# Chunk squares in wider products, router loads, block 0's norms and two Q Grams moved, in a delta-rule attention with top-1 experts

## The chip, the cores and the metric

The kernel runs on one core of one Trainium2 chip. The metric is device time in microseconds, the median of several executions. TensorE does matrix products, VectorE and ScalarE elementwise work and copies out of PSUM, GpSimd (POOL in the profile) masks, copies inside SBUF and indirect DMAs, and SyncE (SP) issues the plain DMAs from one queue, in order.

## The reference, cut to what matters

```
# attention: B, H, S, D = 4, 8, 768, 48
k_n = k / (norm(k) + 1e-06)
state = 0                                   # per (b, h): D x D
for t in range(S):
    y[:, :, t] = q_t @ state                # einsum 'bhd,bhde->bhe'
    v_old = state^T k_t                     # einsum 'bhde,bhd->bhe'
    state += beta_t * outer(k_t, v_t - v_old)
# mixture of experts on x = y as (3072 tokens, 384 features); E = 8 experts, F = 1024
logits = x @ w_gate;  e = argmax(logits);  gate = softmax(logits)[e]
out = gate * (relu(x @ w1[e]) @ w2[e])
```

## The kernel before, in words

The sequence is cut into six blocks of 128 positions; a block of one batch entry is a chunk, numbered n = 4 * block + batch, 24 in all, each with eight heads. `kt_t[n]` holds the keys of a chunk by feature, two heads above each other (rows 0 and 64), and `qt_t[n]` the queries.

For each chunk, `kpart(n)` (L229) forms the Gram of keys (`halves`, L265: eight products with 64 rows and 128 columns, one per head, into two PSUM tiles of the ring "g", which has three buffers) and ScalarE copies both to `gg` (L253). `qpart(n)` (L275) does the same with keys and queries, and GpSimd then masks the result `pm` (L282). Inside a chunk the delta rule is solved in four sub-blocks of 32 positions, for which the 32x32 diagonal blocks of the Gram of all 32 batch-head pairs are inverted at once on VectorE: `prepare(tb)` (L301) takes the squared norms (`squares`), the root on ScalarE (`root`, L298) and the scaling, and `lanes(tb)` (L357) runs the columns of the inverse, then products and reductions (L393, L399), and a last transpose to `wt`. Blocks 1 to 5 get their diagonals by way of DRAM (`gd`, `lg`), from the Grams. Block 0 can't wait for that: the first step of `kpart` for chunks 0 to 3 computes its diagonal blocks alone, the squares, with 32 products of 32 columns for each chunk (L246), which VectorE and ScalarE copy to `dg` (L248, L249), each taking the heads of one half.

Then come 27 ticks. In tick t, `residual(t)` subtracts from the scaled values `v_all` what the states and the earlier sub-blocks give (L434, L446 on TensorE, L453 on VectorE), `apply(t)` multiplies with `wt` (L461), ScalarE copies the result to `u` (L465), and `finish(t - 3)` updates the state and emits the output of a finished chunk, whose tokens go through the router's columns of `esel` (L528). Between these, `beside(t, i)` puts a measured portion of the later blocks' inverses on VectorE; one more K Gram (chunk t + 12) and one Q Gram are formed in each tick. `norms(tb)` (L338) brings the norms into `nt_all`, one column for each head, and `scale_v(t)` (L409) scales a tick's values with them. The experts' products follow behind the ticks and fill the rest of the time.

The order on each engine is that of the program text: the schedule is written by hand. Ahead of the ticks (L869 and after) it is: loads of chunks 0 to 3, dummy products, the steps in `INIT` (first steps of chunks 0 to 3, one step of block 0's `prepare`, the Gram of chunk 0), `constants()` on GpSimd, which ends with the four loads of the router's weights into `esel` (L103), then the loads of chunks 4 to 10 and of values on the same queue, the rest of `prepare(0)`, and the Grams in the order of `FILL`, between which stand the columns of block 0's inverse, `norms(0)` and `scale_v(0)`.

Of the kernel before, what the change touches and what calls it, by code (L numbers as in the profile page):

```python
# [8 lines left out]
F32 = mybir.dt.float32  # L9
# [9 lines left out]
B, H, S, D = 4, 8, 768, 48  # L19
C = 128  # L20
NT = S // C
NB = C // 32
BH = B * H
NP = H // 2
# [17 lines left out]
def deltanet_moe(ctx, tc, kt_d, qt_d, kn_d, v_d, beta_d, w_gate, w1, w2, out):  # L42
    nc = tc.nc
# [27 lines left out]
    def iota(t, pattern, start, step=0):  # L71
        nc.gpsimd.iota(t, pattern=pattern, base=start, channel_multiplier=step, allow_small_or_imprecise_dtypes=True)

    def constants():
        nc.gpsimd.memset(esel, 0.0)
        for p in range(NP):
            for a in range(2):

                r = slice(64 * a, 64 * a + D)
                nc.gpsimd.tensor_copy(esel[r, p, (p + a) % 2 * D:((p + a) % 2 + 1) * D], ident[r, r])  # L80
        cmask = lp.tile([128, 128], F32, name="cmask", tag="u", bufs=UB)
        nc.gpsimd.memset(cmask, 1.0)
        nc.gpsimd.affine_select(out=cmask, in_=cmask, compare_op=ALU.is_gt, fill=0.0, base=0,
                                pattern=[[1, 128]], channel_multiplier=-1)
        nc.gpsimd.tensor_copy(ltri, cmask)
        nc.gpsimd.memset(ones, 1.0)
        iota(last_i, [[1, CAP - 128 * NG]], 128 * NG)
        iota(rev_e, [[-1, E]], E)
        for e in range(E):
            nc.gpsimd.memset(pow_e[:, e:e + 1], float(2 << (E - 1 - e)))  # L90
        iota(base, [[CAP, E]], 0)
        iota(lim, [[CAP, E]], CAP)
        iota(beyond, [[N - CAP, E]], OFF)
        nc.gpsimd.memset(jump, 0.0)
        for i, g in enumerate((G0, NG)):
            nc.gpsimd.memset(jump[:, i, 0:1], float(128 * g))
        iota(ids, [[-C, B * NT]], int(TOPID), -1)
        nc.gpsimd.memset(ids2, 0.0)
        nc.gpsimd.tensor_copy(ids2[:, :, 0], ids)
        wv = w_gate.rearrange("(p a r) e -> a r p e", p=NP, a=2)  # L100
        for a in range(2):
            for o in range(2):
                nc.sync.dma_start(out=esel[64 * a:64 * a + D, o::2, 2 * D:], in_=wv[(a + o) % 2, :, o::2])  # L103

    YB = 2
    KSB = 1
    VA = NT * B - B
    GB = 3
# [7 lines left out]
    NB_ = 2  # L116
    LIVE = 7
    LAG = NB - 1
    FILL = 'k4 k5 k6 k7', 'k1 q0 k2 k3', 'k8 k9', 'k10 k11 q1'

    ROOT = {1: (-1, -1, -1), 2: (17, 20, 22), 3: (38, 41, 43), 4: (66, 69, 71), 5: (94, 97, 99)}
    INIT = (0, 1, 2, 3, 'l', 0)

    STEPS = (3, 3, 3, 2, 2, 2, 2)

# [29 lines left out]
    pss = lp_.enter_context(tc.tile_pool(name="pss", bufs=1, space=PSUM))  # L155
    pg_ = lp_.enter_context(ExitStack())
    psg_ = [pg_.enter_context(tc.tile_pool(name="psg", bufs=GB, space=PSUM))]
# [13 lines left out]
    nt_t = lp.tile([128, (NT * B + LAG) * H], F32, name="nt_all")  # L171
# [16 lines left out]
    def load_rows(t, src, whole):  # L188

        for r in (slice(0, 128),) if whole else (slice(0, D), slice(64, 64 + D)):  # L190
            nc.sync.dma_start(out=t[r], in_=src[r])

    def load_k(n):
        if n < NT * B:
            load_rows(kt_t[n % KTL], kt_d[n], n < KTL)
# [10 lines left out]
    def stage(t):  # L206

        return [(q, t - q) for q in range(NB) if 0 <= t - q < NT * B]
# [20 lines left out]
    def kpart(n):  # L229

        tb, b = n // B, n % B
        kt, gg = kt_t[n % KTL], gg_t[n % KSL]
        V, A = nc.vector.tensor_copy, nc.scalar.copy
        if tb == 0:
            if n == 0:
                tiles["dg"] = fp.tile([128, BH, 32], F32, name="dg", tag="lg", bufs=3)
            dg = tiles["dg"]
            db = [psg_[-1].tile([128, NP, 32], F32, name=f"db{b}_0", tag="g"),
                  pss.tile([128, NP, 32], F32, name=f"db{b}_1", tag="y", bufs=YB) if b < 2 else
                  pss.tile([128, NP, 32], F32, name=f"db{b}_1", tag=f"sum{b - 2}")]  # L240
            for h in range(H):
                p, a = h // 2, h % 2
                r = slice(64 * a, 64 * a + 64)
                for i in range(NB):
                    t = slice(32 * i, 32 * i + 32)
                    nc.tensor.matmul(db[a][t, p, :], lhsT=kt[r, p, t], rhs=kt[r, p, t], start=True, stop=True,  # L246
                                     tile_position=(64 * a, 32 * i), skip_group_check=True)
            V(out=dg[:, b * H:(b + 1) * H:2], in_=db[0])  # L248
            A(out=dg[:, b * H + 1:(b + 1) * H:2], in_=db[1])  # L249
            yield  # L250
        pg = halves(f"pg{tb}_{b}", kt, kt)
        for a in range(2):
            A(out=gg[:, a:H:2], in_=pg[a])  # L253
        if tb > 0 and b == B - 1:
            early_ = CL[tb] if tb < len(CL) else (0, 0)
            clear_slots(early_[0])
            for i in range(NB):
                r = slice(32 * i, 32 * i + 32)
                nc.sync.dma_start(out=gd[tb].rearrange("(i n) (r c) -> i r n c", i=NB, r=32)[i],
                                  in_=gg_g[tb % (KSL // B)].rearrange("p b h c -> p (b h) c")[r, :, r])  # L260
            tiles[tb]["lg"] = fp.tile([128, 32, 32], F32, name=f"lg{tb}", tag="lg", bufs=3)
            clear_slots(early_[1])
            nc.sync.dma_start(out=tiles[tb]["lg"].rearrange("p r c -> p (r c)"), in_=gd[tb])
# [73 lines left out]

    def norms(tb):  # L338
        s0, s1 = tiles[tb]["s0"], tiles[tb]["r0"]
        if tb > 0:  # L340
            nc.vector.transpose(out=s1, in_=s0)
        for q in range(NB):
            p = slice(32 * q, 32 * q + 32)
            c = slice((B * tb + q) * H, (B * tb + q) * H + 32)
            if tb > 0:
                nc.gpsimd.tensor_copy(nt_t[p, c], s1[p])
            else:
                nc.vector.transpose(out=nt_t[p, c], in_=s0[p])
        yield

    def both_halves(t):
# [57 lines left out]
    def scale_v(t, act=False):  # L409

        vn = vt[t]
        for r in rows(t):
            for h in range(H if act else 0):
                nc.scalar.activation(out=vn[r, h], in_=vn[r, h], func=AF.Copy, scale=nt_t[r, t * H + h:t * H + h + 1])
            if act:
                continue
            nc.vector.tensor_tensor(out=vn[r], in0=vn[r], in1=nt_t[r, t * H:(t + 1) * H].unsqueeze(2)
                                    .broadcast_to([r.stop - r.start, H, D]), op=ALU.mult)
# [9 lines left out]
    def residual(t):  # L428

        ks = tiles["ks", t] = pss.tile([128, H, D], F32, name=f"ks{t}", tag="ks", bufs=KSB)  # L430
        st = stage(t)
# [37 lines left out]
    def finish(n):  # L469
# [4 lines left out]
        qt, pm = qt_t[n % QTL], pm_t[n % QSL]  # L474
        yp = [pss.tile([128, NP // 2, C], F32, name=f"yp{tb}_{b}_0", tag="y", bufs=YB),
              psg_[-1].tile([128, NP // 2, C], F32, name=f"yp{tb}_{b}_1", tag="g")]
# [47 lines left out]
    def emit_x(n, yt, row, rl):  # L524

        xp = pss.tile([128, NP, 2 * D + E], F32, name=f"xp{n // B}_{n % B}", tag="y", bufs=YB)
        for p in range(NP):
# [20 lines left out]
    def emit_slots(tb, b, w, row, rl):  # L548
# [28 lines left out]
        for _ in range(FP if w > 1 else 3):  # L577
            yield
        pp = pss.tile([128, w + 1, E], F32, name=f"pp{tb}_{b}", tag="y", bufs=YB)
        nc.tensor.matmul(pp[:, 0:w, :], lhsT=ltri, rhs=ohb, start=True, stop=False, skip_group_check=True)  # L580
# [42 lines left out]
    def pool_slots(tb, b, w, row, rl):  # L623
# [39 lines left out]
        for _ in range(FP):  # L663
            yield
        pp = pss.tile([128, w + 1, E], F32, name=f"pp{tb}_{b}", tag="y", bufs=YB)
        nc.tensor.matmul(pp[:, 0:w, :], lhsT=ltri, rhs=ohb, start=True, stop=False, skip_group_check=True)
# [42 lines left out]
    def dummy(k):  # L709

        if k:
            wm = pss.tile([128, 512], F32, name=f"wm{next(cnt)}", tag="y", bufs=YB)
        for _ in range(k):
# [171 lines left out]
    lane = prepare(0)  # L885
    for i in INIT:
        if i == "l":
# [21 lines left out]
    def fill(xs):  # L909
        for x in xs.split():  # L910
            n, part = int(x[1:]), (ks0 if x[0] == "k" else qs0)
            if part[n] and not run(part[n]):
                done.add(x)

    fill(FILL[0])
    load_k(3 * B - 1)
# [3 lines left out]
        load_ku(n)  # L920
    for n in range(LEAD, LEAD + 2):
        load_k(n)
    fill(FILL[1])
    lane = lanes(0)
    run(lane, 12)
    for _ in norms(0):
        pass
    scale_v(0)
    run(lane, 24)
    fill(FILL[2])  # L930
    fill(FILL[3])
    ks_ = [x for i, x in enumerate(ks_) if f"k{i}" not in done]
# [128 lines left out]
    i = 0  # L1061
# [87 lines left out]
    V = nc.vector  # L1149
# [93 lines left out]
    if True:  # L1243
# [3 lines left out]
        V = nc.vector  # L1247
# [61 lines left out]
        for f in range(KF):  # L1309
# [4 lines left out]
                                     in_=yo, in_offset=None, bounds_check=N - 1, oob_is_err=False)  # L1314
# [40 lines left out]
```

## Time and profile before

| | |
|---|---|
| median of 3 runs | 496.92 us (496.26 to 499.41) |
| the profiled execution | 496.72 us, span 495.0 us |
| TensorE, products | 453.5 us busy (92%), 7212 |
| TensorE, weight loads | 417.3 us busy (84%), 7212 |
| VectorE | 323.8 us busy (65%), 726 |
| ScalarE | 262.1 us busy (53%), 566 |
| GpSimd | 166.1 us busy (34%), 338 |
| mean granted clock of TensorE | 0.982 |
| DMA | 73.33 MB, mean 148 GB/s |

The span is what the profiler saw of the program from its first to its last instruction; the execution's own time is 1.72 us longer. Busy time is a share of the whole span and hides that the stages have different limits. In rows of a timeline the first number is the start in microseconds from the start of the span, the second the time that the row covers, xN the number of instructions that it merges, and the bracket the idle time of the engine ahead of it with what ended it. A single-precision product appears as two instructions, so the 128 squares of four chunks make 256.

### The profile page before, as it was taken

What the parts mean: (1) busy time and instruction counts of PE and PEld (TensorE: products, weight loads), DVE (VectorE), ACT (ScalarE), POOL (GpSimd) and SP (SyncE); (2) the same over time, 40 slices, a digit from 0 to 9 for tenths busy, and PEclk for the clock granted to TensorE, in tenths of its full rate; (3) what the DMA queues carried; (4) which work ended last, traced back from release to release, by engine and by line L of the source; (5) the groups of instructions that cost most, each with busy time, mean ns of one, the idle gap of its engine ahead of it and who ended that gap; (6) DMA issues with size and microseconds to landing.
All of it is one profiled execution on the core that took longest, in us unless ns stands there. A gap on an engine that the chain in (4) does not pass through costs nothing. (4 is left out here: it accounts for less than half of the span.)

```text
span 495.0 us, 17216 instructions
## 1 busy us (share of the span) xinstructions
PE 453.5 (92%) x7212; PEld 417.3 (84%) x7212; DVE 323.8 (65%) x726; ACT 262.1 (53%) x566; POOL 166.1 (34%) x338
## 2 busy tenths in 40 slices
PE   6866799999999899978899999999999999999995
PEld 4755678887888687866798999999999999999995
DVE  3899998899889989446544767373463647255330
ACT  3464767675756466766433455463553545364230
POOL 7013123768888878730311210201102020201111
PEclk9998889999999999999999899999999999999999
DMA  5999478575384243734302548474545547353101
GB/s 164 246 291 252 126 156 254 169 162 168 88 206 106 86 131 89 234 121 128 101 35 66 168 139 248 140 223 132 177 124 171 175 150 199 138 170 106 36 3 46
DMA packets 57147, 73.33 MB, mean 148 GB/s; under 512 B 25929, under 2 KB 44831, under 8 KB 57056
## 3 DMA queue, kind: packets, MB, share of 16 engines
q1 hardware_dynamic: 53600, 62.44, 44.4%
q0 software_dynamic: 3456, 9.57, 5.3%
q8 instruction: 71, 1.16, 1.0%
q14 instruction: 20, 0.16, 0.1%
HBM read 54.15 MB, written 18.62 MB: 147 GB/s over the span
## 5 line engine op out<-in xcount | busy, mean ns | idle before, releaser
L801 POOL DMA_INDIRECT out_dram<-yo,idx x32 | 30.7, 959 | 198.7 <-ACT yo L1134 100.8
L798 PE MATMUL y<-w2h,hx 128*128 128x384 f32 x352 | 93.5, 340 | 0.1
L721 DVE TENSOR_TENSOR w2l<-w2r,w2h 128x768 fp32r<-128x768 f32 x32 | 31.2, 979 | 73.3 <-ACT w2h L720 73.2
L798 PEld LDWEIGHTS y<-w2h,hx 128*128 128x128 f32 x352 | 64.1, 188 | 0.4 <-issue 0.4
L798 PE MATMUL y<-w2l,hx 128*128 128x384 f32 x176 | 59.3, 337 | 0.0
L787 PE MATMUL h<-xl,w1h 128*128 128x416 f32 (+2 forms) x168 | 57.2, 341 | 0.2 <-DVE xl L721 0.2
L787 PE MATMUL h<-xh,w1h 128*128 128x416 f32 (+2 forms) x168 | 57.3, 341 | 0.0
L787 PE MATMUL h<-xh,w1l 128*128 128x416 f32 (+2 forms) x168 | 57.2, 340 | 0.0
L465 ACT COPY u<-ks 32x384 f32<-32x384 f32 x96 | 45.1, 469 | 21.0 <-PE ks L461 18.4
L282 POOL TENSOR_SCALAR_AFFINE_SELECT pm<-pm 128x1024 f32<-128x1024 f32 x24 | 27.1, 1130 | 75.9 <-ACT pm L281 75.5
L790 ACT ACTIVATE hx<-h 128x448 fp32r<-128x448 f32 (+1 forms) x64 | 32.9, 517 | 32.8 <-PE h L787 32.0
L1134 ACT ACTIVATE yo<-y,gt 128x384 f32<-128x384 f32 x22 | 12.8, 581 | 69.1 <-PE y L798 57.9
L434 PE MATMUL ks<-st,kt 128*32 128x96 f32 x768 | 45.1, 253 | 2.5 <-ACT u L465 2.1
L791 DVE SCALAR_TENSOR_TENSOR hx<-h,hx 128x448 fp32r<-128x448 f32 (+1 forms) x64 | 36.8, 587 | 14.5 <-ACT hx L790 14.4
L271 PE MATMUL pg<-kt 64*128 64x128 f32 x384 | 34.0, 319 | 8.0 <-DMA kt<-in_kt_dram 4.3
L271 PEld LDWEIGHTS pg<-kt 64*128 64x128 f32 x384 | 28.8, 219 | 12.4 <-ACT gg L253 6.4
L434 PEld LDWEIGHTS ks<-st,kt 128*32 128x32 f32 x768 | 33.2, 111 | 6.1 <-ACT u L465 2.6
L253 ACT COPY gg<-pg 128x512 f32<-128x512 f32 x48 | 25.8, 589 | 23.8 <-PE pg L271 23.8
L536 POOL DMA_INDIRECT xg<-row,sli x24 | 29.2, 1216 | 25.7 <-ACT yt L508 8.0
L461 PE MATMUL ks<-v_all,wt 32*32 32x48 f32 x1536 | 25.9, 203 | 12.9 <-DVE v_all L453 10.7
L461 PEld LDWEIGHTS ks<-v_all,wt 32*32 32x32 f32 x1536 | 21.3, 105 | 17.8 <-DVE v_all L453 12.6
L721 DVE TENSOR_TENSOR w1l<-w1r,w1h 128x1024 fp32r<-128x1024 f32 x24 | 29.4, 1224 | 9.8 <-ACT w1h L720 6.6
(197 smaller groups left out, 1040.5 us busy)
## 6 DMA issues: line engine op xcount, KB each, us to landing
w1r<-in_w_dram SPq DMA_DIRECT2D x24, 512.0 KB
w2r<-in_w_dram SPq DMA_DIRECT2D x32, 384.0 KB
xg<-zrow SPq DMA_DIRECT2D x7, 788.0 KB
kt<-in_kt_dram SPq DMA_DIRECT2D x17, 256.0 KB
xr<-xg SPq DMA_DIRECT2D x7, 591.0 KB
ku<-in_kn_dram SPq DMA_DIRECT2D x20, 192.0 KB
qt<-in_qt_dram SPq DMA_DIRECT2D x36, 96.0 KB
v_all<-in_v_dram SPq DMA_DIRECT2D x15, 192.0 KB
```

The source lines that it names most:

```text
L271: nc.tensor.matmul(pg[a][:, p], lhsT=kt[r, p], rhs=xt[r, p], start=True, stop=True, tile_position=(64 * a, 0), skip_group_check=True)
L282: nc.gpsimd.affine_select(out=pm, in_=pm, compare_op=ALU.is_gt, fill=0.0, base=0, pattern=[[0, H], [1, C]], channel_multiplier=-1)
L434: nc.tensor.matmul(ks[32 * q:32 * q + 32, 2 * p:2 * p + 2, :], lhsT=kt_t[n % KTL][:, p, 32 * q:32 * q + 32], rhs=st_view(n % B, p), start= ...
L461: nc.tensor.matmul(ks[r, h, :], lhsT=tiles[n // B]["wt"][r, n % B * H + h, :], rhs=vn[r, h, :], start=True, stop=True, tile_position=(32 * ...
L465: nc.scalar.copy(out=uview(n)[r], in_=ks[r])
L536: put = nc.gpsimd.indirect_dma_start(out=xg, out_offset=bass.IndirectOffsetOnAxis(ap=at, axis=0), in_=x, in_offset=None, bounds_check=OFF ...
L721: nc.vector.tensor_tensor(out=lo, in0=src, in1=hi.bitcast(F32), op=ALU.subtract)
L787: nc.tensor.matmul(ps, lhsT=w[:, d, fs], rhs=x_[:, d], start=(n == 0), stop=(n == len(terms) - 1))
L790: nc.scalar.activation(out=hh, in_=ps, func=AF.Relu)
L791: nc.vector.scalar_tensor_tensor(out=hl, in0=ps, scalar=0.0, in1=hh.bitcast(F32), op0=ALU.max, op1=ALU.subtract)
L798: nc.tensor.matmul(ps, lhsT=h(f)[h_], rhs=w2[w][:, f, :], start=(n == 0), stop=(n == len(terms) - 1))
L801: nc.gpsimd.indirect_dma_start(out=out, out_offset=bass.IndirectOffsetOnAxis(ap=idx, axis=0), in_=yo, in_offset=None, bounds_check=N - 1, ...
```

## The change

Five edits:

- The squares of chunks 0 and 1 are formed by 16 products of 64 columns for each chunk; chunks 2 and 3 keep 32 of 32 columns. The wider tiles hold more than the diagonal blocks, so these are copied out by four copies of 32 rows on VectorE and four on ScalarE instead of one and one.
- The router's four loads leave `constants()` and are issued after the loads of chunks 12 and 13.
- In `INIT`, `prepare(0)` makes three steps (transpose, squares, root) ahead of the Gram of chunk 0, instead of one.
- Block 0's norms go as the other blocks' do: one transpose on VectorE and four copies on GpSimd, instead of four transposes on VectorE. The first scaling of values is done by eight operations on ScalarE instead of one on VectorE.
- Q Grams 0 and 1 leave `FILL`. `qs_` still lists them, so each is formed where the ticks take Q Grams: after `beside(t, 5)` of ticks 0 and 1.

```diff
@@ -97,12 +97,15 @@
         iota(ids, [[-C, B * NT]], int(TOPID), -1)
         nc.gpsimd.memset(ids2, 0.0)
         nc.gpsimd.tensor_copy(ids2[:, :, 0], ids)
+
+    def router():
         wv = w_gate.rearrange("(p a r) e -> a r p e", p=NP, a=2)
         for a in range(2):
             for o in range(2):
                 nc.sync.dma_start(out=esel[64 * a:64 * a + D, o::2, 2 * D:], in_=wv[(a + o) % 2, :, o::2])
 
     YB = 2
+    WIDE = 2
     KSB = 1
     VA = NT * B - B
     GB = 3
@@ -116,10 +119,10 @@
     NB_ = 2
     LIVE = 7
     LAG = NB - 1
-    FILL = 'k4 k5 k6 k7', 'k1 q0 k2 k3', 'k8 k9', 'k10 k11 q1'
+    FILL = 'k4 k5 k6 k7', 'k1 k2 k3', 'k8 k9', 'k10 k11'
 
     ROOT = {1: (-1, -1, -1), 2: (17, 20, 22), 3: (38, 41, 43), 4: (66, 69, 71), 5: (94, 97, 99)}
-    INIT = (0, 1, 2, 3, 'l', 0)
+    INIT = (0, 1, 2, 3, 'l', 'l', 'l', 0)
 
     STEPS = (3, 3, 3, 2, 2, 2, 2)
 
@@ -235,18 +238,22 @@
             if n == 0:
                 tiles["dg"] = fp.tile([128, BH, 32], F32, name="dg", tag="lg", bufs=3)
             dg = tiles["dg"]
-            db = [psg_[-1].tile([128, NP, 32], F32, name=f"db{b}_0", tag="g"),
-                  pss.tile([128, NP, 32], F32, name=f"db{b}_1", tag="y", bufs=YB) if b < 2 else
-                  pss.tile([128, NP, 32], F32, name=f"db{b}_1", tag=f"sum{b - 2}")]
+            w = 64 if b < WIDE else 32
+            db = [psg_[-1].tile([128, NP, w], F32, name=f"db{b}_0", tag="g"),
+                  pss.tile([128, NP, w], F32, name=f"db{b}_1", tag="y", bufs=YB) if b < 2 else
+                  pss.tile([128, NP, w], F32, name=f"db{b}_1", tag=f"sum{b - 2}")]
             for h in range(H):
                 p, a = h // 2, h % 2
                 r = slice(64 * a, 64 * a + 64)
-                for i in range(NB):
-                    t = slice(32 * i, 32 * i + 32)
+                for i in range(0, C, w):
+                    t = slice(i, i + w)
                     nc.tensor.matmul(db[a][t, p, :], lhsT=kt[r, p, t], rhs=kt[r, p, t], start=True, stop=True,
-                                     tile_position=(64 * a, 32 * i), skip_group_check=True)
-            V(out=dg[:, b * H:(b + 1) * H:2], in_=db[0])
-            A(out=dg[:, b * H + 1:(b + 1) * H:2], in_=db[1])
+                                     tile_position=(64 * a, i), skip_group_check=True)
+            for i in range(0, w, 32):
+                for t in range(i, C, w) if w > 32 else (slice(0, C),):
+                    t = t if w == 32 else slice(t, t + 32)
+                    V(out=dg[t, b * H:(b + 1) * H:2], in_=db[0][t, :, i:i + 32])
+                    A(out=dg[t, b * H + 1:(b + 1) * H:2], in_=db[1][t, :, i:i + 32])
             yield
         pg = halves(f"pg{tb}_{b}", kt, kt)
         for a in range(2):
@@ -337,15 +344,11 @@
 
     def norms(tb):
         s0, s1 = tiles[tb]["s0"], tiles[tb]["r0"]
-        if tb > 0:
-            nc.vector.transpose(out=s1, in_=s0)
+        nc.vector.transpose(out=s1, in_=s0)
         for q in range(NB):
             p = slice(32 * q, 32 * q + 32)
             c = slice((B * tb + q) * H, (B * tb + q) * H + 32)
-            if tb > 0:
-                nc.gpsimd.tensor_copy(nt_t[p, c], s1[p])
-            else:
-                nc.vector.transpose(out=nt_t[p, c], in_=s0[p])
+            nc.gpsimd.tensor_copy(nt_t[p, c], s1[p])
         yield
 
     def both_halves(t):
@@ -920,12 +923,13 @@
         load_ku(n)
     for n in range(LEAD, LEAD + 2):
         load_k(n)
+    router()
     fill(FILL[1])
     lane = lanes(0)
     run(lane, 12)
     for _ in norms(0):
         pass
-    scale_v(0)
+    scale_v(0, act=True)
     run(lane, 24)
     fill(FILL[2])
     fill(FILL[3])
```

## Rows read from the trace of the kernel before

**Rows 1.** Busy time by stretch: stretch, its length, then each engine, clock, DMA.

```profile
20.00:40.00 20.00, 13.58 (x182) 11.48 (x182) 19.32 (x31) 11.35 (x22) 2.90 (x2) 1.00 0.95 274
...
48.00:55.00 7.00, 5.54 (x123) 4.93 (x126) 6.42 (x21) 3.46 (x13) 0.00 (x0) 0.76 1.03 266
...
62.00:70.00 8.00, 7.39 (x210) 6.45 (x211) 8.00 (x13) 5.94 (x18) 0.31 (x1) 0.79 0.60 100
70.00:80.00 10.00, 9.70 (x256) 8.58 (x255) 8.07 (x30) 6.15 (x14) 4.69 (x9) 1.00 0.99 280
```

**Rows 2.** Timeline of TensorE, ticks 0 to 3.

```profile
38.94 1.16 PE L271 MATMUL pg<-kt 64*128 64x128 f32 x16 [1.39 <-DMA kt<-in_kt_dram]
...
44.98 2.02 PE L271 MATMUL pg<-kt 64*128 64x128 f32 x16
48.06 0.87 PE L461 MATMUL ks<-v_all,wt 32*32 32x48 f32 x32 [1.05 <-DVE v_all L453]
49.99 1.31 PE L434 MATMUL ks<-st,kt 128*32 128x96 f32 x16 [1.06 <-ACT u L465]
...
52.84 1.53 PE L271 MATMUL pg<-kt 64*128 64x128 f32 x16
...
62.61 0.88 PE L461 MATMUL ks<-v_all,wt 32*32 32x48 f32 x64 [2.03 <-DVE v_all L453]
```

**Rows 3.** Timeline of VectorE from the start to tick 3.

```profile
8.93 0.29 DVE L248 COPY dg<-db 128x128 f32<-128x128 f32 x1 [1.80 <-PE db L246]
...
12.28 0.35 DVE L317 RECIPROCAL r<-s 128x32 f32<-128x32 f32 x1 [0.78 <-ACT s L299]
...
18.24 0.86 DVE L348 STREAM_TRANSPOSE nt_all<-s 32x32 f32<-32x32 f32 x4
19.12 0.55 DVE L417 TENSOR_TENSOR v_all<-v_all,nt_all 32x384 f32<-32x384 f32 x1
...
24.96 3.19 DVE L393 TENSOR_TENSOR big<-lg 128x1024 f32<-128x1024 f32 x2
...
32.26 2.30 DVE L393 TENSOR_TENSOR big<-lw,lg 128x1024 f32<-128x1024 f32 x2
...
38.55 0.32 DVE L295 TENSOR_SCALAR ss<-lg 128x32 f32<-128x32 f32 x1
...
54.12 0.54 DVE L453 TENSOR_TENSOR v_all<-v_all,ks 96x384 f32<-96x384 f32 x1
...
57.79 0.18 DVE L295 TENSOR_SCALAR ss<-lg 128x32 f32<-128x32 f32 x1
...
59.94 2.15 DVE L393 TENSOR_TENSOR big<-lw,lg 128x1024 f32<-128x1024 f32 x1
```

**Rows 4.** Timeline of TensorE, the squares.

```profile
3.65 1.58 PE L246 MATMUL db<-kt 64*32 64x32 f32 x128
5.97 1.20 PE L246 MATMUL db<-kt 64*32 64x32 f32 x90 [0.74 <-DMA kt<-in_kt_dram]
8.34 0.68 PE L246 MATMUL db<-kt 64*32 64x32 f32 x38 [1.17 <-issue]
```

**Rows 5.** DMA queues between 5 and 6 us: packets, MB, share of 16 engines.

```profile
q8 instruction: 1, 0.02, 7.2%
```

**Rows 6.** Timeline of ScalarE ahead of and in tick 0.

```profile
12.01 0.24 ACT L299 ACTIVATE s<-ss 128x32 f32<-128x32 f32 x1
...
42.49 1.91 ACT L414 ACTIVATE v_all<-v_all,nt_all 64x48 f32<-64x48 f32 x8
```

**Rows 7.** Timeline of GpSimd, masks of Q Grams 0 and 2.

```profile
25.33 1.81 POOL L282 TENSOR_SCALAR_AFFINE_SELECT pm<-pm 128x1024 f32<-128x1024 f32 x1 [14.92 <-ACT pm L281]
...
59.92 1.09 POOL L282 TENSOR_SCALAR_AFFINE_SELECT pm<-pm 128x1024 f32<-128x1024 f32 x1 [14.41 <-ACT pm L281]
```

**Rows 8.** Timeline of the DMA queue: issues ahead of tick 0.

```profile
5.41 2.81 SPq L103 DMA_DIRECT2D esel<-in_w_gate_dram  x4
...
33.70 1.01 SPq L191 DMA_DIRECT2D kt<-in_kt_dram  x2
```

## The prediction

> **What bounds the kernel now.** I read the table of busy time by stretch first, then the timeline of VectorE from the start to 65 us, then those of TensorE, ScalarE, GpSimd and the DMA queue around it. The reader is to see that every edit lies ahead of tick 2, that is in the first 60 us of 495, and that VectorE is what ends last there: it is busy 19.32 of the 20 us before the ticks and 6.42 of 7 us in ticks 1 and 2, with TensorE at 13.58 and 5.54 [rows 1]. Up to tick 3 TensorE waits for VectorE: its products of tick 3 start at 62.61 after 2.03 us of idle that VectorE's subtraction ends [rows 2]. From there on TensorE is full (7.39 of 8 us, then 9.70 of 10) and VectorE has holes (8.07 of 10) [rows 1]. So a microsecond taken off VectorE's chain before 62 us starts all that follows a microsecond earlier, and one taken off TensorE, ScalarE or the queue there is worth nothing unless it releases VectorE. The base of the sum is the profiled execution, 496.72 us (span 495.0); it stands 0.20 under the median of the runs, 496.92.
>
> **Squares (minus 1.3).** VectorE's chain starts when the last diagonal block is copied, at 8.93, after 1.80 us of idle [rows 3]. Chunk 3's products are cut in two: 90 products go out from 5.97 without a break, then come 1.17 us of idle that the profile puts to "issue", then the last 38 [rows 4]. The cut is in the middle of one chunk, where no product waits for anything, so I take it for instructions that had not been fetched: up to there TensorE had 128 + 90 products with as many weight loads, at 12 to 13 ns each [rows 4], and one block of 16 KB of instructions moved between 5 and 6 us [rows 5]. The change leaves 192 of these 256 products, so the cut falls behind the squares, into the Grams, which nothing on VectorE waits for. Chunk 3 is then copied at about 7.6 instead of 8.93; I take the idle of 1.17 and the shorter stream together as 1.3. Bounds: 0, if the cut is no fetch, to 1.4. What a 64-column product costs no row shows. By the issue pace of the 32-column ones (1.58/128 = 12 ns) 32 take 0.4 us a chunk; by the Gram's 128-column ones at the slow clock (2.02/16 = 0.126 us [rows 2], half the columns, twice as many array tiles at work) 1.0 us. I take 1.0, the nearer shape, and it is covered: two chunks end at 3.65 + 2.0 = 5.7, and chunk 2 waits for its load until 5.97 [rows 4]. The six more copies on VectorE and on ScalarE cost at most 0.29 each, as the whole one does [rows 3]; chunk 1's end at about 7.2 and chunk 2's single copy follows by 7.5. Should the load of chunk 2 come earlier, up to 0.4 us of them would show.
>
> [...]
>
> **Root ahead of the Gram's copies (minus 0.5).** VectorE stands idle 0.78 before the reciprocal at 12.28 [rows 3], because ScalarE first makes chunk 0's two Gram copies and starts the root at 12.01; it takes 0.24 [rows 6]. With the root first the idle is some 0.3. The copies slip behind it, and chunk 4's Gram, which needs their buffers, still gets them earlier, since the root itself comes 1.3 earlier.
>
> **Norms and first scaling (minus 1.1).** Four transposes (0.86) and the product (0.55) hold VectorE from 18.24 on, 1.41 of which some 0.1 overlaps; one transpose of all partitions stays, some 0.2 (a quarter of the four) [rows 3]. GpSimd's four copies stand in a queue that is empty for 14.92 us before 25.33 [rows 7]. The new wait is ScalarE's: eight scalings, 1.91 [rows 6], wait for those copies and stand ahead of chunk 8's Gram copies. The norms are there by 19, and Q Gram 0, which has chunks 2 and 3 behind it, is masked only at 25.33 [rows 3, 7], so ScalarE does not wait. The Gram stream loses 1.9 us and gets back two Q Grams of 1.16 and more; at its end it waits for loads anyway (1.39 at 38.94 [rows 2]). Price nothing; without that cover 1.9 us, on TensorE.
>
> **Q Grams (minus 1.0, then plus 1.8).** The mask of Q Gram 0 on GpSimd begins at 25.33 and lasts until 27.14 [rows 7], and VectorE's pair of products there takes 3.19 us where the same pair at 32.26 takes 2.30 [rows 3]: 0.89 lost, as one of the two engines stands still. Gram 1's mask meets reductions and costs 0.14 (0.32 at 38.55 against 0.18 for the same small operation at 57.79). Both go. In ticks 0 and 1 they come back in front of a VectorE that is just as full: at the end of each tick's queue the mask meets the two-operand products of the inverse's columns. The third mask, at 59.92, shows the price: a product of 2.15 us that should take some 1.2, the larger of a pair of 2.30 [rows 3, 7]. I take 0.9 each, bounds 0 (beside a reduction) and 1.1 (the mask's own 1.09). TensorE's 1.16 and ScalarE's 1.07 a Gram go into holes: 0.61 after tick 0's products, 1.05 and 1.06 in tick 1 [rows 2].
>
> **Router's loads (0).** Four loads of 2.81 us of the queue's time, issued at 5.41, held the chunk loads behind them to 8.22 [rows 8]. Without them the loads of chunks 4 to 10, v and q go out some 5 us earlier, and the first Grams start with their buffers, as much earlier as the root, 1.5 to 2 us. Moved behind the loads of chunks 12 and 13 at 33.70 [rows 8], the four stand in front of block 2's diagonal and of the ticks' loads. That pushes these against the ticks by up to 2.8 us; the queue reaches them at some 37 all the same, the first reader of block 2's diagonal on VectorE is at 57.79 [rows 3], and the router's own first product comes in tick 3. Chunk 12's load, for which TensorE waits at 38.94 [rows 2], hangs on block 1's diagonal and so on the Grams; it comes about 1.5 to 2 us earlier, less than VectorE's 3.9, which tick 0's slack on TensorE takes up.
>
> **The sum.** 1.3 + 0.5 + 1.1 + 1.0 = 3.9 off ahead of tick 0, 1.8 given back in ticks 0 and 1: 2.1 off, 496.72 - 2.1 = **494.6** (0.5% under the median).
>
> **The rivals.**
> *The masks miss.* If they fall beside reductions or subtractions from PSUM, the 1.8 is not paid: 492.8; and if the third mask, too, misses its 2.15 us product, 491.9. For it: the copies queue behind ScalarE's eight scalings, so the hour is loose. Against it: VectorE in ticks 0 and 1 is mostly two-operand work.
> *The cut stays.* If the 1.17 us is no fetch, or the new early loads hold up the fetch or chunk 3, 1.3 is lost: 495.9.
> *Slower: TensorE at half clock in ticks 0 and 1.* With the Q Grams out, TensorE idles longer before tick 0. [...] If chunk 12's load does not come earlier than 38.94 and the clock is at the low level, then: its Gram ends at 40.96; chunk 13's starts at 44.98 - 0.20 + 2.02 - 0.61 = 46.2; chunk 14's 7.86 later, less the wait of 1.05, plus 2.02 - 1.06, at 54.0 [rows 2]. Tick 2's subtraction, at 54.12 before [rows 3], then gains nothing of the 3.9, and the second mask's 0.9 is paid behind it: 497.5. It decides once the low level lasts through both ticks; against it, dense work there should raise the clock again, as it did by tick 2's end.
> *Nothing arrives.* The same absorption without the mask: 496.6.
>
> **How the numbers follow.** The forecast has 0.45 (its own range 493.8 to 495.5), the masks that miss 0.20, the cut that stays 0.15, the slower one 0.15, nothing 0.05. About 1%, 5 us, is what a measurement of this kernel can tell from no change. Below 491.9 lies only the far end of the first rival with a favourable clock behind it: 0.08 for faster; slower by 5 us has no case that I can price: 0.03; the same 0.89. The range takes in the rivals: 491.9 to 497.6.
>
> **What would show it.** Squares: one unbroken run of chunks 2 and 3 and the last diagonal copy by 7.7; a cut in a Gram instead. Root: under 0.35 of idle before the first reciprocal. Norms: one 0.2 us transpose, and all that follows it on VectorE 2.9 earlier, 3.9 by the start of tick 0. Masks: two VectorE products in ticks 0 and 1 that last about 1 us too long. Ticks: the products of tick 3 near 60.5 instead of 62.61, and still TensorE idle before them. I am wrong if that idle is gone, if the clock stays low past tick 1, or if what arrives at tick 3 does not arrive at the end.

## The result, and the profile after

The median of 22 runs is 500.95 us (497.29 to 505.27) against 498.0 us (494.44 to 505.81) of 22 runs of the kernel before beside them: the ratio on record, which leaves out one slow run of each kernel and isn't the plain quotient of the medians, is 1.0054, with an interval of 1.0030 to 1.0078. So the change costs about half a per cent where half a per cent of gain was forecast. The profiled execution after took 499.45 us (span 497.7), 2.73 us more than the one before; its mean granted clock is 0.962.

I read the timeline of VectorE first, because the forecast hung on it. The columns are those of [rows 3]; in the lines after, helpers stand some lines lower (L456 is the subtraction of L453, L396 the product of L393). The last line is from a window behind the others.

```profile
8.10 1.93 DVE L316 STREAM_TRANSPOSE lg<-dg 128x1024 f32<-128x1024 f32 x1
...
10.75 0.35 DVE L324 RECIPROCAL r<-s 128x32 f32<-128x32 f32 x1 [0.30 <-ACT s L306]
...
16.71 0.20 DVE L347 STREAM_TRANSPOSE r<-s 128x32 f32<-128x32 f32 x1
...
22.22 2.29 DVE L396 TENSOR_TENSOR big<-lg 128x1024 f32<-128x1024 f32 x2
...
38.30 0.54 DVE L456 TENSOR_TENSOR v_all<-v_all,ks 32x384 f32<-32x384 f32 x1 [1.32 <-DMA kt<-in_kt_dram]
...
45.53 0.71 DVE L377 TENSOR_TENSOR tmp<-lg,lw 128x128 f32<-128x128 f32 x1
...
50.37 1.12 DVE L380 TENSOR_TENSOR lw<-lw,tmp 128x30 f32<-128x30 f32 x1
...
58.95 1.23 DVE L396 TENSOR_TENSOR big<-lw,lg 128x1024 f32<-128x1024 f32 x1
...
121.81 0.55 DVE L456 TENSOR_TENSOR v_all<-v_all,ks 128x384 f32<-128x384 f32 x1 [3.60 <-PE ks L449]
```

At first the reader sees the forecast. The wait ahead of the reciprocal has gone from 0.78 to 0.30, one transpose of 0.20 stands where four took 0.86, and the pair of products that lost to the mask takes 2.29 instead of 3.19 [rows 3]. Two small operations in ticks 0 and 1 take 0.71 and 1.12 (their neighbours of the same shapes 0.29 and 0.19): they meet the moved masks, which GpSimd starts at 44.90 and 50.36 and which take 1.20 and 1.09. Two things differ from the forecast. Tick 0's subtraction stands idle for 1.32 us ahead of 38.30; the bracket names a load, but the subtraction starts just behind TensorE's products for it (36.72 in the next fence), which end at 38.21. And the third mask misses the product that it slowed before (58.95, 1.23 instead of 2.15 [rows 3]). Tick 3's subtraction comes 1.91 us earlier than before, that of tick 9 still 2.17 earlier (111.07 against 113.24). That of tick 10 comes at 121.81, 0.66 later than before, after 3.60 us of idle. So 2.83 us go in one tick, far behind every edit. TensorE tells how, in the timeline of the kernel after:

```profile
3.66 1.99 PE L250 MATMUL db<-kt 64*64 64x64 f32 x64
5.90 0.82 PE L250 MATMUL db<-kt 64*32 64x32 f32 x64 [0.26 <-DMA kt<-in_kt_dram]
6.98 0.75 PE L250 MATMUL db<-kt 64*32 64x32 f32 x64 [0.25 <-DMA kt<-in_kt_dram]
...
13.01 1.22 PE L278 MATMUL pg<-kt 64*128 64x128 f32 x8 [1.06 <-issue]
...
36.72 1.49 PE L437 MATMUL ks<-st,kt 128*32 128x96 f32 x8
...
60.70 0.88 PE L464 MATMUL ks<-v_all,wt 32*32 32x48 f32 x64 [0.64 <-DVE v_all L456]
...
112.84 0.45 PE L487 MATMUL yp<-qt,st 64*64 64x128 f32 x8
115.60 0.71 PE L487 MATMUL yp<-qt,st 64*64 64x128 f32 x8 [2.31 <-issue]
```

In the same timeline of the kernel before, tick 0's products took 0.85, and those of the last two lines ran through in one:

```profile
36.70 0.85 PE L434 MATMUL ks<-st,kt 128*32 128x96 f32 x8
...
115.78 0.67 PE L484 MATMUL yp<-qt,st 64*64 64x128 f32 x16
```

The squares of chunk 3 are whole now, and the products of tick 3 start at 60.70, against 62.61 before [rows 2] and 60.5 in the forecast. But 16 equal products of tick 9, which wait for nothing, are cut in two by 2.31 us. Busy time by stretch, with the granted clock third from the end, shows what follows:

```profile
112.50:115.50 3.00, 0.79 (x48) 0.57 (x37) 2.83 (x11) 2.68 (x7) 1.57 (x5) 0.98 0.81 248
115.50:118.80 3.30, 3.20 (x40) 2.67 (x39) 2.71 (x3) 0.72 (x3) 2.46 (x6) 0.50 0.12 19
```

Behind the cut the granted clock stands at 0.50 for 3.3 us, and then comes back (1.00 from 118.8 on). In the 3 us around the cut the DMA engines are 0.81 busy; an instruction block starts to move at 113.06, and TensorE starts again 2.5 us later. Behind tick 10 the shift stays between -0.4 and +0.8 until tick 20; two more cuts, 1.72 at 206.49 and 1.23 at 211.84, lie ahead of +0.9 and +2.0 in ticks 21 and 22, and +1.0 is left in the last tick. The rest up to 2.7 at the end arises behind the ticks; there the clock is low for 6.8 us from 275.8 on instead of 3.4 from 275.5, and what else adds to it was not followed up.

**Where the cuts stand.** I counted TensorE's recorded instructions (products and weight loads) from the start to each idle stretch of over 0.5 us whose next product waits for nothing. In the 18 profiles of this study there are 80 of them, 0.52 to 4.06 us long, and all stand within 12 of the counts 446, 699, 953 and so on in steps of 253.4. The cut of chunk 3's squares stands at 447, the one in tick 9 at 4492. A packet of the instruction queue (q8) carries 16 KB (71 packets, 1.16 MB in the kernel before); I take the step of 253.4 for one such block. The wider squares take 64 products away, 128 recorded instructions (14296 instead of 14424): half a step. So every later border falls on another point of the program.

The packets of the instruction queue fit this: while TensorE passes 25 of these borders in the kernel before, from 85 to 197 us, 25 of them start. For a cut, the packet that counts is the first behind the border one step earlier. In all 80 cases TensorE goes on 2.2 to 3.2 us after it. In the kernel before TensorE passes the border ahead of tick 9's at 109.51 and the packet starts at 110.29; in the kernel after it passes at 109.27, and the packet starts at 113.06, too late. What goes with the delay can be seen in the microsecond behind the passing: the DMA engines were over half busy in 78 of the 80 cases. Of the 324 passings behind which they were under 0.2 busy, none led to a cut.

### The profile page after: what moved, and what is told of

It is laid out like the page before. It is cut to its first block, busy times and chain, and to the rows that moved or that the text cites. A ratio compares the mean times of both kernels' runs of the same rounds, so it can differ in the third digit from the quotient of the medians.

```text
span 497.7 us, 17116 instructions
## 1 busy us (share of the span) xinstructions
PE 455.4 (92%) x7148; PEld 420.0 (84%) x7148; DVE 326.2 (66%) x728; ACT 265.6 (53%) x580; POOL 165.7 (33%) x342
## 5 line engine op out<-in xcount | busy, mean ns | idle before, releaser
L278 PE MATMUL pg<-kt 64*128 64x128 f32 x384 | 36.5, 337 | 9.9 <-ACT gg L260 6.7
L437 PE MATMUL ks<-st,kt 128*32 128x96 f32 x768 | 43.8, 251 | 1.7 <-issue 1.7
L278 PEld LDWEIGHTS pg<-kt 64*128 64x128 f32 x384 | 31.0, 235 | 14.5 <-ACT gg L260 9.5
L260 ACT COPY gg<-pg 128x512 f32<-128x512 f32 x48 | 25.7, 587 | 23.2 <-PE pg L278 23.2
L464 PE MATMUL ks<-v_all,wt 32*32 32x48 f32 x1536 | 24.8, 205 | 10.8 <-DVE v_all L456 10.1
```

The costliest lines, as they stand in the source:

```text
L278: nc.tensor.matmul(pg[a][:, p], lhsT=kt[r, p], rhs=xt[r, p], start=True, stop=True, tile_position=(64 * a, 0), skip_group_check=True)
L437: nc.tensor.matmul(ks[32 * q:32 * q + 32, 2 * p:2 * p + 2, :], lhsT=kt_t[n % KTL][:, p, 32 * q:32 * q + 32], rhs=st_view(n % B, p), start= ...
L464: nc.tensor.matmul(ks[r, h, :], lhsT=tiles[n // B]["wt"][r, n % B * H + h, :], rhs=vn[r, h, :], start=True, stop=True, tile_position=(32 * ...
```

## The experiments

Ratios are to the kernel before in runs on the same chip, 22 runs of the change, 12 of each other kernel (6 of e8, one each of e15 and e16). "Block" is the start of the first packet of the instruction queue; "cuts" is the sum of TensorE's idle stretches of over 0.25 us whose next product waits for nothing, in the whole span; "tick 3" is the shift of that tick's subtraction against the profile before. These three are of one profiled execution each.

| kernel | ratio | block | cuts | tick 3 |
|---|---|---|---|---|
| before | 1 | 5.7 | 4.7 | 0 |
| after | 1.0054 [1.0030, 1.0078] | 10.1 | 7.3 | -1.9 |
| e1 after, 32 products in tick 2 | 1.0016 [0.9982, 1.0050] | 9.6 | 5.6 | +0.6 |
| e2 before, the same | 1.0052 [1.0014, 1.0090] | 6.6 | 5.6 | -0.6 |
| e3 after, narrow squares | 1.0028 [0.9988, 1.0068] | 8.9 | 10.6 | +3.2 |
| e4 before, wide squares | 1.0045 [1.0007, 1.0084] | 6.8 | 7.2 | -2.2 |
| e5 after, products spread | 1.0031 [0.9995, 1.0067] | 9.1 | 2.8 | -2.8 |
| e6 before, the same | 1.0070 [1.0037, 1.0102] | 6.2 | 6.8 | 0.0 |
| e7 after, Q Grams back | 1.0008 [0.9976, 1.0039] | 10.2 | 8.6 | -3.6 |
| e8 after, fewer loads | 1.0151 [1.0109, 1.0194] | 9.5 | 6.8 | -2.5 |
| e9 after, router back | 0.9969 [0.9931, 1.0008] | 7.3 | 5.6 | -2.6 |
| e10 e9, products spread | 0.9942 [0.9905, 0.9978] | 7.1 | 4.3 | -0.2 |
| e11 e10, Q Grams back | 0.9946 [0.9913, 0.9979] | 7.1 | 6.6 | -4.2 |
| e12 before, norms and root alone | 0.9958 [0.9920, 0.9997] | 5.8 | 3.5 | -2.1 |
| e13 after, router in both places | 1.0027 [0.9990, 1.0063] | 6.8 | 6.5 | -1.8 |
| e14 after, router in tick 1 | 1.0057 [1.0024, 1.0090] | 11.8 | 10.5 | 0.0 |
| e15, e16 after again, one run each | | 11.5, 9.5 | 8.3, 7.1 | -0.3, -0.8 |

### The count of instructions: e1 to e6

The theory: borders decide. 32 single-precision products of zeros are 128 recorded instructions; they bring the borders behind them back to where they were before (e1), or, put into the kernel before, move its borders by half a block (e2).

```diff
+    def pad(k):
+        ...
+            nc.tensor.matmul(wm[o:o + 32, 0:32], lhsT=zrow[r, 0:32], rhs=zrow[r, 0:32], ...)
+        if t == 2:
+            pad(32)
```

> The changed kernel with 32 extra zero products (128 instructions on TensorE, nobody reads their result) in tick 2, where TensorE waited 1.75 us for a load. Theory F (instruction fetch): the wider squares take 128 instructions out of TensorE's stream, which moves every later border of its 16 KB instruction blocks; in tick 9 a border now falls where the DMA engines are full, the block comes late, TensorE stands 2.31 us and the clock falls. With the count put back from tick 2 on, that gap is gone and the ratio to the kernel before is 0.994 to 1.000. Rival Q (Q Grams and clock): the loss comes from the two Q Grams and TensorE's clock in the first ticks and arrives late; the ratio stays at 1.003 to 1.008.

> The kernel before with the same 32 zero products in tick 2 and nothing else. 128 more instructions put the borders of the blocks where 128 fewer put them. F: from tick 2 on it stalls where the changed kernel does, a gap of 1 to 2.5 us in tick 9 or near it, ratio 1.004 to 1.010. Q: the products cost at most their own 0.8 us beside a TensorE that waits in tick 3, ratio 0.998 to 1.002.

In e1 the cut of tick 9 is gone and the span is 494.3, but a new one stands right behind the burst, at the border of count 1458 (e3, below, has 2.47 at the same border without a burst). The line is of TensorE's timeline in e1:

```profile
57.52 1.86 PE L278 MATMUL pq<-qt,kt 64*128 64x128 f32 x13 [2.80 <-issue]
```

In e2 the border comes into tick 9 of a kernel that has none of the edits, 0.82 and 0.91 at 109.84 and 114.91, and the kernel is slower by 0.5%. The products themselves take 1.08 us and go into TensorE's wait for VectorE (tick 3 is no later, -0.6). So a burst that adds nothing but instructions costs as much as the change. e1's ratio lies between what the theory (at most 1.000) and its rival (at least 1.003) asked for. e3 and e4 take the squares alone: out of the change, and alone into the kernel before.

```diff
-    WIDE = 2
+    WIDE = 0
```

> The changed kernel with 32-column products for all four chunks; the other four edits stay. F: TensorE has as many instructions as before, the borders are back, no gap in tick 9; about 1 us of the squares' gain is lost; ratio 0.995 to 1.001. Q: still 1.003 to 1.008.

> The kernel before with the wider squares of chunks 0 and 1 alone. F: the start gains 1.3 us, the gap of tick 9 costs 2 to 3 us and its clock, ratio 1.002 to 1.008. Q: only the gain, ratio 0.996 to 0.998.

e4 gains 2.2 us by tick 3 and is slower at the end (1.0045), with cuts of 1.56 at 109.65, 1.34 at 151.30 and 1.69 at 211.35: the wide squares alone show a loss of the same size. e3 gave more than I had asked for, and its ratio, too, lies between the two theories. Up to the squares its order on TensorE is that of the kernel before, and still the cut in chunk 3's squares has grown from 1.17 [rows 4] to 4.06; timeline of TensorE in e3:

```profile
6.02 1.17 PE L250 MATMUL db<-kt 64*32 64x32 f32 x90 [0.88 <-DMA kt<-in_kt_dram]
11.25 0.67 PE L250 MATMUL db<-kt 64*32 64x32 f32 x38 [4.06 <-issue]
```

The border is the same; what differs ahead of it is the DMA queue, from which the router's loads have gone. This opened the question of e9. First the burst was dealt out, one or two products ahead of each portion `beside(t, i)` of ticks 0 to 2, so that no dense stretch of small instructions meets a border.

```diff
+    def spread(t, i):
+        if t > 2:
+            return
...
 in beside(t, i):
+        spread(t, i)
```

> The changed kernel with the 32 zero products dealt out over ticks 0 to 2, one or two ahead of each portion of the inverse, instead of in one burst that uses up 128 instructions at once. F: from tick 3 on every border stands in the same place of the program as in the kernel before, no gap over 1 us in tick 9 or in ticks 20 and 21, and no burst that outruns the fetch in tick 2; tick 3 about 2 us earlier than before and so to the end: ratio 0.994 to 0.999. Q: 1.003 to 1.008 as the change.

> The kernel before with the same products dealt out over ticks 0 to 2. F: borders as in the changed kernel from tick 3 on; gaps in ticks 9 and 20 or 21, the gaps of 'issue' on TensorE add up to some 2 us more than before; ratio 1.003 to 1.008. Q: 0.999 to 1.002.

e5's profiled execution is the fastest of all, 492.4 us (span 490.6), with one cut of 2.18 at 204 and an idle stretch of 1.17 at 159, at a border too, behind a wait that had ended 1.1 us before. Its twelve runs give 1.0031 all the same, which is the rival's number and not the theory's (at most 0.999): the count is not the whole of the loss. e6 is slower than before by 0.7%. Giving the 128 instructions back to the change brings 0.2 to 0.4% (e1, e5; e10 against e9, below, 0.3%), which these intervals don't tell apart from nothing; adding them to the kernel before costs 0.5 and 0.7%, which they do.

What the count decides is plain in tick 9. Of the 18 profiles of this study, eleven are of kernels whose count there is half a block off that of the kernel before; all eleven have a cut of 0.8 to 2.3 us at one of the two borders in or next to it (counts 4239 to 4499). The seven with its count have none of over 0.5 there.

### The masks and the loads in tick 9: e7, e8

```diff
-    FILL = 'k4 k5 k6 k7', 'k1 k2 k3', 'k8 k9', 'k10 k11'
+    FILL = 'k4 k5 k6 k7', 'k1 q0 k2 k3', 'k8 k9', 'k10 k11 q1'
```

> The changed kernel with Q Grams 0 and 1 back ahead of the ticks. F: the count up to tick 2 is the same, so the gap of tick 9 stays; the masks' price changes by less than 1 us: ratio 1.002 to 1.007. Q: the loss goes with them: 0.993 to 0.998.

Tick 3 comes 3.6 us earlier than before, against 1.9 in the change; but two further profiles of the change have 0.3 and 0.8 (e15, e16), so one pair of profiles doesn't price the move. What the trace does show is that the forecast's gain of 1.0 in the fill was not the move's: with the rest of the fill moved, Q Gram 0's mask falls beside a reduction in e7, and the pair of products takes 2.29 without any move of the Gram (VectorE's timeline in e7).

```profile
21.77 2.29 DVE L396 TENSOR_TENSOR big<-lg 128x1024 f32<-128x1024 f32 x2
23.98 1.21 DVE L402 TENSOR_REDUCE lg<-big 128x64 f32<-128x1024 f32 x1
25.23 1.16 DVE L396 TENSOR_TENSOR big<-lg 128x784 f32<-128x784 f32 x1
```

The mask runs from 24.47 for 1.09 on GpSimd; the product behind the reduction loses 0.19 to it (0.97 at 31.81 for the same shape). At the end e7 has 1.0008, below what the theory of borders asked for (1.002 to 1.007) and above its rival's range, with cuts of 1.37, 1.03 and 1.14 at 77, 111 and 116. Its interval and that of the change overlap by 0.0009 only, so the Q Grams' place may carry a part of the loss; e11 against e10, below, shows none.

e8 leaves out the loads of values in ticks 8 and 9, so two of block 3's four parts are not loaded; its results differ, TensorE records 14328 instructions instead of 14296, and its time at the end can't be compared.

```diff
-                if t == B * (tb - 1) + i:
+                if t == B * (tb - 1) + i and t not in (8, 9):
```

> The changed kernel without the loads of values in ticks 8 and 9 (two of block 3's four parts are not loaded and old values stand in for them), some 0.4 MB of the 2.7 MB that move while the block of instructions for tick 9 is awaited. F, with the block held up behind data: the gap of 2.31 us in tick 9 shrinks to under 1 us and the subtraction of tick 10 comes at least 1.5 us earlier. If the border alone makes the gap, whatever the DMA engines do, it stays at 2 us or more.

The cut at count 4492 is gone, but one border earlier, at 4239, 1.97 us stand, and tick 10 is 2.25 late instead of 0.66. My expectation failed, and the run shows nothing of the loads' share.

### The router's loads: e9 to e14

```diff
-    def router():
...
-    router()
```

> The changed kernel with the router's four loads back ahead of the loads of chunks 4 to 10. Theory E (early loads): with them moved, the DMA engines are full from 2 us on, the next blocks of instructions wait behind data already in the squares and in the first Grams and ticks, and that costs some 2 us on average up to tick 3, on top of the border in tick 9. E: tick 3 comes at least 2 us earlier than before, and the ratio is 1.000 to 1.003. If the early loads cost nothing, the ratio stays at 1.004 to 1.008.

With the loads back in their first place the change runs at 0.9969, better than the 1.000 to 1.003 that I had asked for, against 1.0054 with them moved; the intervals don't touch. The stretch from 6 to 9 us shows the difference. The fences are busy time by stretch of the kernels before, after and e9; the last three columns are granted clock, share of the DMA engines, GB/s.

```profile
6.00:9.00 3.00, 1.83 (x130) 1.64 (x130) 0.37 (x2) 0.27 (x1) 2.60 (x19) 1.00 0.09 11
```

```profile
6.00:9.00 3.00, 2.75 (x146) 2.46 (x146) 2.64 (x8) 1.52 (x6) 2.60 (x19) 1.00 1.12 382
```

```profile
6.00:9.00 3.00, 2.83 (x138) 2.73 (x140) 2.49 (x8) 1.51 (x6) 2.60 (x19) 1.00 0.13 18
```

The router's four loads have 3.0 KB each and hold the queue for 2.81 us [rows 8]; while they do, the DMA engines are all but idle (0.09, 0.13). Through this hole the first instruction block comes, at 5.7 and 7.3. Without it the chunk loads fill the engines (1.12), and the block comes at 10.1, seen in the DMA queues between 10 and 11 us of the kernel after (columns as in [rows 5]):

```profile
q1 hardware_dynamic: 47, 0.18, 94.6%
q8 instruction: 1, 0.02, 8.6%
```

e10 adds the spread products to e9, e11 takes the Q Grams back too; their edits stand above.

> The same with the 32 zero products dealt out over ticks 0 to 2, so that the borders from tick 3 on are those of the kernel before. E and F together: no gaps that the kernel before has not, ratio 0.994 to 0.999. If something else eats the gain, 1.000 to 1.004.

> The same with the two Q Grams back as well: of the change only the wider squares, the root's place, the norms and the first scaling are left, and the borders are restored. E and F: 0.992 to 0.998, the best of these. Else 0.999 to 1.003.

Both beat both kernels: 0.9942 and 0.9946. Against e5, e10 differs in the router's place alone and gains 0.9% again. (By the plain quotients of the medians both steps, e9 against the change and e10 against e5, are 0.7%.) The Q Grams' place makes no difference between them that can be measured, though tick 3 lies 4 us apart in their profiles.

e12 makes only the edits that touch neither the count on TensorE nor the loads.

```diff
-    INIT = (0, 1, 2, 3, 'l', 0)
+    INIT = (0, 1, 2, 3, 'l', 'l', 'l', 0)
...
-    scale_v(0)
+    scale_v(0, act=True)
```

> The kernel before with the root's place, the norms and the first scaling alone: TensorE's instructions and all loads as before. Every theory: 1.5 us off VectorE's chain, tick 3 comes 1.2 to 1.8 us earlier. F: it reaches the end, ratio 0.995 to 0.998. If a gain ahead of the ticks is lost whatever the borders do, 0.999 to 1.003.

Its tick 3 starts 2.1 us earlier, by TensorE's timeline, and every tick up to 8 is 2.1 to 2.5 earlier, the last tick 2.4, the end 2.3:

```profile
60.51 1.06 PE L457 MATMUL ks<-v_all,wt 32*32 32x48 f32 x64 [2.03 <-DVE v_all L449]
```

So a microsecond taken off VectorE's chain does arrive at the end (0.9958). Two last kernels ask whether the loads hurt by the hole that they leave or in the place where they go: in both places (e13), and moved on behind the loads of tick 1 (e14).

```diff
 e13, in constants():
+    router()
 e14:
-    router()
...
+        if t == 1:
+            router()
```

> The changed kernel with the router's four loads issued in both places, the old and the new. Theory H (the hole): in the old place they keep the queue from loading ahead of 8 us, so the DMA engines are free when TensorE's next block of instructions is asked for; moving them filled that hole. H: ratio 0.995 to 1.001, and the first block moves before 8 us. Theory L (the new place): four times 96 small pieces stand in front of block 2's diagonal and the ticks' loads, and that costs the time: 1.003 to 1.008.

> The changed kernel with the router's loads neither in the old nor in the new place, but behind the loads of tick 1, when the DMA engines are about to run empty. H: the hole at 6 to 9 us stays filled, the first block moves at 9 us or later, ratio 1.003 to 1.008. L: nothing stands in front of the ticks' loads, ratio 0.995 to 1.000.

e14 is as slow as the change, 1.0057, with the loads out of both places; its first block comes at 11.8 and the first cut is 3.12 us, in the Gram stream (TensorE's timeline):

```profile
14.65 1.44 PE L278 MATMUL pg<-kt 64*128 64x128 f32 x9 [3.12 <-issue]
```

That speaks for the hole, unless the third place has a price of its own. e13 keeps the hole, has its block at 6.8 and no cut in the first 65 us, as expected, but ends at 1.0027 where the hole alone asked for 0.995 to 1.001. It differs from e9 only by the loads in the new place, and is 0.6% slower; from the change only by the hole, and is 0.3% faster. By the intervals the first difference is uncertain by some 0.5% and the second by some 0.4%. So a part of the price, perhaps the larger, may lie in the new place; how the two divide stays open.

> The changed kernel once more, to see which of its gaps come again. H and F: the first block of instructions moves at 9 us or later, tick 3 comes anywhere from 4 us earlier to 3 us later, and the gap sizes at the borders differ, but they stand at the same instructions.

> The changed kernel a third time, for the same question: the first block of instructions at 9 us or later, tick 3 from 4 us earlier to 3 us later than before, the gaps at the same instructions with other sizes.

The two further profiles of the change (spans 501.2 and 500.3) have cuts at the borders in tick 9's neighbourhood both times, 1.29 at 111.8 and 0.94 at 111.6, one border earlier than the first profile's 2.31, followed by 0.55 and 1.10 at 117, at its border. So the borders are the kernel's. Which of them is cut and how long is the execution's: the early cut is 1.36, 0.85 and 1.06, and tick 3 is 0.3, 0.8 and 1.9 earlier.

## Why the prediction was wrong

Two terms failed: the squares, priced at minus 1.3, and the router's loads, priced at nothing. The time, 500.95, lies above the whole range of 491.9 to 497.6.

**The reading of the base** holds but for one wait. VectorE bounds the first 62 us, and what is saved there starts the ticks earlier: tick 3 by 1.91 in the change, 2.1 in e12, where it reaches the end. That the sum of 2.1 up to tick 3 was met within 0.2 (60.70 against 60.5) is luck; the two further profiles of the change have 0.8 and 0.3. VectorE's work for block 0 did end 3.75 earlier (36.98 against 40.73), near the 3.9 of the sum. Then three things stood against each other: 1.32 of wait in tick 0, for TensorE, which the forecast had at nothing; the two masks at 1.35 instead of 1.8; and 0.92 won by the third mask.

**Squares** failed in its second half. It said that the cut is instructions not yet fetched; that is borne out by the counts (80 cuts of 80 at the steps of 253.4) and by the packets (TensorE goes on 2.2 to 3.2 us after one in all 80), and the squares did come out whole (the wide ones of two chunks in 1.99, for which 2.0 was taken). It then let the cut fall "behind the squares, into the Grams, which nothing on VectorE waits for", as if there were one cut. There is a border every 253.4 recorded instructions to the end of the kernel, and what takes 128 instructions away moves them all. From tick 3 on TensorE is full [rows 1], so a cut there is late for everything: 2.31 us in tick 9 and the low clock behind it (0.50 for 3.3 us) took back what the prologue had gained. What the Gram's cut itself (1.06) cost can't be told: behind it and a wait of 2.21 for ScalarE's copies the clock stood at 0.50 from 13.0 to 23.2, where the kernel before has full clock until 43.4. e4, with the squares alone, has the gain by tick 3 (-2.2) and, instead of 0.3% of gain at the end, 0.45% of loss; e2 and e6 have the loss without any edit but the count.

**The rival that the cut stays.** The first cut stands at the first border in both kernels (count 447 before), and so it moved out of the squares into a Gram. Of the 999 borders in the 18 profiles 80 show a cut of over 0.5 us, of 0.52 to 4.06 each. My chance for this rival was a chance against the wrong thing: the cut did move.

**Router's loads (0)** is mis-sized, and the larger of the two terms: 0.85% by e9, some 4 us, 0.9% by e10 against e5. I looked for what the moved loads would push away, priced that at nothing, and priced the earlier chunk loads as no loss. What these took was the hole in which the DMA engines had time for instructions; the block that came at 5.7 comes at 10.1. That this hole is what costs the 4 us is not shown: e13 leaves a part, perhaps the larger, to the new place. A half-sentence of a rival, that "the new early loads hold up the fetch", had this at 1.3 us and by the squares only.

**Root, norms, first scaling** were right in mechanism and sum (0.30 against "some 0.3"; one transpose of 0.20). e12 has -2.1 for these edits alone, where 1.6 was said; 0.3 of it is its smaller cut in the squares, 0.88 instead of 1.17.

**Q Grams** were right in kind: the masks met VectorE's work in ticks 0 and 1, for 0.42 and 0.93 (0.71 less 0.29, 1.12 less 0.19) where 0.9 each was said, and the pair in the fill is free of its mask. The traces show the masks as the forecast took them: before, the pair with the mask beside it lasts 3.19, against 2.30 for the same pair alone and 1.09 for a later mask [rows 3, 7]; after, a subtraction from PSUM at 130.00 takes its 0.55 and a reduction at 185.38 its 1.21, each beside a mask (129.85 to 130.96, 185.34 to 186.42). But e7 shows that the gain in the fill was due to the hour and not to the Gram's place. Of the slower rival, TensorE at half clock, a piece is there in this profile: the clock was 0.5 from 30.1 to 40.3, TensorE's products for tick 0 took 1.49 instead of 0.85 and ended at 38.21, so the subtraction waited 1.32 for them (38.30), and chunk 12's Gram behind them took 1.95. TensorE was busy for 9.28 of those 10.2 us; in tick 2 of the kernel before it was busy for all of the 3.4 us at 0.50 (50.2 to 53.6), and 1.00 followed. Ticks 1 to 3 did not lose by it what that rival asked for.

**The chances.** The range was too narrow on the slow side since no case priced TensorE behind tick 3. Adding up the parts, 0.45% by e4 and 0.85% by e9, less 0.42% by e12, gives 0.9% of loss without the Q Grams; 0.5% was measured, inside what the intervals (some 0.4% each way for each part) allow.

## What to carry to other kernels

Ahead of adding or removing instructions on a long unrolled queue, count where its fetch borders stand (from the counts of cuts that nothing releases; here every 253.4 recorded instructions) and look at what lies at each border after the edit, above all where that engine is full and the DMA engines too (over half busy at 78 of the 80 cuts here). A stretch in which the DMA engines are idle can be what lets instructions through (here 0.09 to 0.15 busy from 6 to 9 us, with the first packet at 5.7 to 7.3): before filling it with early loads, look for the instruction packets in it. And judge such an edit with its count given back and its loads left in place, one at a time, on several executions: a sum that fits one profile up to the edit's own stage to 0.2 us can do so by errors that cancel, and the end can be decided elsewhere.

## What was not expected of the hardware

- Idle stretches of TensorE of 0.52 to 4.06 us that no wait explains stood only at steps of 253.4 recorded instructions (80 of 80). TensorE went on 2.2 to 3.2 us after the block's packet starts (5.74 to 8.34 before, 8.87 to 11.25 in e3, 113.06 to 115.60 after).
- Blocks came late where the DMA engines were full of data: the first at 8.9 to 11.8 us in the nine profiles with the router's loads away from their first place (the DMA engines 0.97 to 1.12 busy from 6 to 9 us), at 5.7 to 7.3 in the nine with them there (0.09 to 0.15). With the engines under 0.2 busy no crossing of a border led to a cut (0 of 324), with them over half busy 78 of 582 did.
- 128 instructions that compute nothing needed made the kernel before slower by 0.52% [0.14, 0.90] and 0.70% [0.37, 1.02].
- A cut of 2.31 us was followed by a granted clock of 0.50 for 3.3 us.
